# Two of the last block's four half-width output stores moved from SyncE's DMA queue to GpSimd's

## The chip, the cores and the metric

The kernel runs on one core of one Trainium2 chip. The metric is the device time of one launch in microseconds; the figure given for a kernel is the median over several runs. A change of about 0.2% (0.46 us here) is what a measurement of this kernel can tell from none.

## What is computed

A pooled attention is followed by a feed-forward layer with three maxed branches. q, k and v have the shape (8, 8, 576, 64); the reference comes down to this:

```python
k_p = k.reshape(B, H, Sp, pool, D).mean(axis=3)      # pool = 8, Sp = 72
v_p = v.reshape(B, H, Sp, pool, D).mean(axis=3)
attn = softmax(q @ k_p.T / sqrt(D))
x = (attn @ v_p).transpose(0, 2, 1, 3).reshape(4608, 512)
h = max(x @ w1, x @ w2, x @ w3)                      # 4608 x 768
out = h @ w_out                                      # 4608 x 512, float32
```

The change concerns only how part of `out` gets from SBUF to DRAM.

## The kernel before, in words

The 4608 tokens are worked through in nine blocks of 512 (NB). For each block the attention of the image it falls in gives `xT`, the hidden layer gives `hT` (the first branch is subtracted from the two others and added back later through `wm`, so that two products and a max remain), and a projection gives `out`. Blocks 0 to 5 use plain matmuls (`hidden`, line 363, and `project`, line 381). From block 6 on the hidden layer is computed by a scheme with seven products instead of eight on half-size pieces (`seven`, line 698). For the last block, block 8 (`LAST`), the projection is also done by seven products instead of eight (`out_seven`, line 638), at the very end of the kernel; it treats the block's 512 tokens as two halves j = 0 and 1 of 256, each in two groups of 128 tokens, m = 0 and 1.

The order of instructions is written out by hand: each engine runs its own queue in the order in which the program issues to it, and an instruction waits on semaphores for its inputs. DMAs to DRAM are issued by whichever engine's queue the program names: `nc.sync` (SyncE, "SPq" in the profile), `nc.scalar` (ScalarE's queue, "ACTq") or `nc.gpsimd` (GpSimd, "POOL").

The end of the program (lines 802 to 812) is this. Of the plain projection's tiles (blocks 5 to 7, 128 tokens each) two steps are taken first (lines 804 and 805), which end one such tile. Then `fold_h` makes sums of pieces of `hT`, and `outs(i, m)` runs fourteen products in the order given on line 808. Each product is five accumulating matmuls (line 670) into PSUM tiles `oA`, `oB` or `oC`. Products 1, 5, 6 and 3 are copied to the SBUF tile `ob` (called `o` in the code) by ScalarE (`copy`, line 675); products 2, 4 and the pair 5 and 7 are added onto it by VectorE (`plus`, line 678). `ob` is 128 partitions by 2 token halves j, by 2 groups m, by 512 columns of float32. When all that feeds a piece is there, `store` (line 645) sends it out, in two DMAs, one for partitions 0 to 63 (u = 0) and one for 64 to 127 (u = 1), since the two halves go to different rows of `out`:

- "lo": j = 0, columns 0 to 255, after product (2, 1), issued from GpSimd (line 686): two DMAs of 128 KB.
- "j1": j = 1, all 512 columns, after product (3, 1), issued from SyncE (line 694): two DMAs of 256 KB.
- "hi": j = 0, columns 256 to 511, after product (4, 1), issued from SyncE (line 690): two DMAs of 128 KB. These are the two that the change moves.

After the fourteen products the rest of `tiles` runs (line 811): the last plain projection tile (`last` on line 385), cut into two column halves. The first half ("c0") is copied from PSUM to `osb` by ScalarE (line 400), the second ("c1") by VectorE (line 398), and each is stored by two DMAs of 64 KB: u = 0 from SyncE's queue, u = 1 from ScalarE's (line 404). The kernel's last instructions, on line 838, wait on SyncE for every DMA semaphore, one wait after another, and then bring all engines together in a barrier that GpSimd collects.

The SyncE and ScalarE DMAs take their completion semaphore from one set of eight in turn, GpSimd's from another set of eight.

Of the kernel before, what the change touches and what calls it, by code (L numbers as in the profile page):

```python
# [14 lines left out]
def kernel(  # L15
# [11 lines left out]
    nc = tc.nc  # L27
# [34 lines left out]
    def psum(shape, dtype, name, tag, bufs):  # L62
        return pools[-1].tile(shape, dtype, name=name, tag=tag, bufs=bufs)
# [529 lines left out]
    def turns(n):  # L593
        return (pad3 if n % 2 else pad)[:, 0:4]
# [16 lines left out]
    def out_w(z, r):  # L611

        i, j = divmod(z, 2)
        c = slice(HALF * i, HALF * i + HALF)
        return wm_sb[:, 2 * j + r, c] if r < 2 else wo_sb[:, JH * j + r - 2, c]

    def out_s(z):
        return so["S4"][:, 0:5] if z == 4 else so["S123"][:, 5 * z - 5:5 * z]
# [19 lines left out]
    def out_seven(n):  # L638

        o = sb2.tile([128, 2304], F32, name="ob", tag="et")[:, 0:2048].rearrange(  # L640
            "p (j m c) -> p j m c", j=2, m=2)
        lo, hi = slice(0, HALF), slice(HALF, C)
        banks, done = {}, set()

        def store(e, j, c):
            for u in range(2):
                b, g = divmod(2 * (4 * n + 2 * j) + u, NG)
                dst = out[S * b:S * b + S, :].rearrange("(r g) c -> r g c", g=NG)
                e.dma_start(out=dst[:, GS[g]:GS[g + 2] + 1:4, c],
                            in_=o[64 * u:64 * u + 64, j, :, c])  # L650

        def product(i, m):
            of = "B" if i == 2 else "C" if i in (4, 7) else "A"
            if i in FIRST:
                tag = {"A": PA, "B": SC, "C": BC if m == 0 else SC}[of]
                banks[of, m] = psum([128, 2, HALF], F32, name=f"o{of}", tag=tag[0],
                                    bufs=tag[1])
            p = banks[of, m][:, 0]
            za, zb = PRODUCTS[i]
            for r in range(5):  # L660
                c = slice(128 * m, 128 * m + 128)
                if isinstance(zb, str):
                    z = int(zb[1]) - 1
                    left = turns(n)[:, z, r, c] if r < 2 else th[n][:, z, r - 2, c]
                else:
                    at = HALF * (zb % 2) + 128 * m
                    left = (xT[:, 2 * (zb // 2) + r, NB * n + at:NB * n + at + 128] if r < 2
                            else hTs[n][:, JH * (zb // 2) + r - 2, at:at + 128])
                right = out_s(int(za[1]))[:, r] if isinstance(za, str) else out_w(za, r)
                nc.tensor.matmul(p, left, right, start=(i in FIRST and r == 0), stop=(r == 4),  # L670
                                 skip_group_check=True)
            done.add((i, m))

            def copy(j, c):
                nc.scalar.copy(out=o[:, j, m, c], in_=p)

            def plus(j, c, p):
                nc.vector.tensor_tensor(out=o[:, j, m, c], in0=o[:, j, m, c], in1=p,
                                        op=ALU.add)

            if i in (1, 5, 6, 3):
                copy(i in (5, 3), lo if i in (1, 3) else hi)
            elif i == 2:
                plus(0, lo, p)
                if m:
                    store(nc.gpsimd, 0, lo)
            elif i == 4:
                plus(0, hi, p)
                if m:
                    store(nc.sync, 0, hi)  # L690
            if i in (5, 7) and (12 - i, m) in done:
                plus(1, hi, banks["C", m][:, 0])
            if i in (5, 7, 3) and all((z, m) in done for z in (5, 7, 3) for m in range(2)):
                store(nc.sync, 1, slice(0, C))

        return product
# [146 lines left out]
```

The softmax here doesn't subtract the row's maximum and nothing guards it: scores larger than these inputs give would overflow.

## Time and profile before

| what | value |
|---|---|
| median of 5 runs | 230.79 us (230.74 to 231.25) |
| the profiled execution itself | 230.88 us |
| its span in the profile | 229.2 us (229.17 in the trace); 1.7 us lie around it |
| TensorE busy | 218.9 us, 96% of the span |
| GpSimd (POOL) busy | 140.0 us, 61%; nothing between 201.8 and 218.2 us |
| DMA queue q0 (GpSimd), q1 (SyncE), q10 (ScalarE) | 16.98, 16.13 and 0.13 MB |
| stores of `ob` | two from POOL, four from SyncE |
| stores at line 404 | 62 of 128 KB from SyncE; at the end two of 64 KB from SyncE and two from ScalarE |

Times in the profile are in us from the start of the span, of one execution. "PE" is TensorE, "DVE" VectorE, "ACT" ScalarE, "POOL" GpSimd, "SPq" and "ACTq" the queues of SyncE and ScalarE that issue DMAs. The time of a DMA instruction on a queue is the time for which it holds that queue; the bytes move later, and the DMA has landed when all sixteen DMA engines have raised its semaphore. A wait that ends late is put down to what ended it.

### The profile page before, as it was taken

Reading aid. Unit: us, or ns where it says so; the run is one execution under the profiler, and the core shown is the slowest. Engines: PE = TensorE matmul, PEld = TensorE weight load, DVE = VectorE, ACT = ScalarE, POOL = GpSimd, SP = SyncE. Lnnn points to the kernel's source line nnn. Section 1 sums busy time; section 2 is a strip of 40 time slices with the busy share of each in tenths; the row PEclk is TensorE's granted clock in tenths of the full one; section 3 lists DMA queues with packets and bytes.
Section 4 is the critical chain, followed back from the end, with each engine's and each line's share of the span. In section 5 each row is a group of like instructions: output and inputs, shape, how many; then the busy total and the mean of one; then the engine's idle time right before and its main releaser. Section 6 shows DMA issues by size and latency. Waiting matters only on the chain.

```text
span 229.2 us, 4411 instructions
## 1 busy us (share of the span) xinstructions
PE 218.9 (96%) x1686; PEld 134.5 (59%) x1687; DVE 129.9 (57%) x246; ACT 122.7 (54%) x221; POOL 140.0 (61%) x115
## 2 busy tenths in 40 slices
PE   7688999999999999999999999999999999999992
PEld 2467645558656545544554455455678667786682
DVE  3568876038426333632363236368578887897830
ACT  2277424756864586238623862684776435465330
POOL 7974201999959999999999749900343442920020
PEclk9999999999999999999999999999999999999999
DMA  6999999999569999887998799941421534301336
GB/s 160 212 197 197 209 205 208 199 179 225 104 111 218 225 170 205 155 185 118 224 166 195 122 217 193 190 110 24 92 60 30 122 72 88 82 12 46 74 69 183
DMA packets 47157, 33.52 MB, mean 146 GB/s; under 512 B 27104, under 2 KB 41888, under 8 KB 47136
## 3 DMA queue, kind: packets, MB, share of 16 engines
q0 software_dynamic: 16944, 16.98, 45.8%
q1 hardware_dynamic: 30032, 16.13, 31.5%
q8 instruction: 13, 0.21, 0.4%
q10 hardware_dynamic: 160, 0.13, 0.2%
q14 instruction: 8, 0.07, 0.1%
HBM read 34.60 MB, written 9.44 MB: 192 GB/s over the span
## 4 chain that ended last, share of the span: by engine, by line
PE 83%; DVE 5%; DMA 4%; ACT 3%; issue 2%; POOL 1%; DVEq 0%; ACTq 0%; POOLq 0%
PE pw L346 23%; PE po L395 18%; PE po L391 11%; PE pA L733 6%; PE psc L207 5%; PE pav L255 4%; DMA vt<-in_v_dram 4%; PE pC L733 3%; PE pm L333 2%; PE oA L670 2%; PE pB L733 2%; DVE kz L198 2%; DVE xn L263 2%; ACT kz L198 2%; PE pxt L245 1%
## 5 line engine op out<-in xcount | busy, mean ns | idle before, releaser
L346 PE MATMUL pw<-xT,mw 128*128 128x512 f16 (+1 forms) x336 | 73.1, 348 | 0.4 <-ACT xT L249 0.2
L395 PE MATMUL po<-mwo,hT 128*128 128x512 f16 (+1 forms) x198 | 46.8, 372 | 0.0
L354 DVE TENSOR_TENSOR hT<-t,pw 128x512 f16<-128x512 f16 (+1 forms) x42 | 25.5, 610 | 36.7 <-ACT et L212 19.1
L346 PEld LDWEIGHTS <-mw 128*128 128x128 f16 x336 | 31.6, 98 | 21.5 <-DVE mw L319 0.6
L400 ACT COPY osb<-po 128x512 f32<-128x512 f32 (+1 forms) x32 | 18.6, 580 | 41.2 <-PE po L395 40.3
L212 ACT ACTIVATE et<-psc 72x576 f16<-72x576 f32 (+2 forms) x54 | 35.2, 661 | 7.1 <-PE psc L207 7.0
L151 POOL TENSOR_TENSOR half<-vt 72x2048 f32<-72x2048 f16 x7 | 28.4, 4060 | 13.7 <-DMA vt<-in_v_dram 13.3
L391 PE MATMUL po<-wm,xT 128*128 128x512 f16 (+1 forms) x132 | 33.0, 372 | 0.3 <-ACT osb L400 0.3
L352 ACT ACTIVATE t<-pw 128x512 f16<-128x512 f32 (+1 forms) x42 | 22.6, 537 | 13.3 <-PE pw L346 11.5
L263 DVE TENSOR_TENSOR xn<-pav,rcp 128x512 f16<-128x512 f32 x40 | 27.7, 692 | 1.6 <-DVE rcp L261 0.2
L395 PEld LDWEIGHTS <-hT 128*128 128x128 f16 x198 | 18.5, 98 | 16.3
L152 POOL TENSOR_TENSOR half<-half 72x1024 f32<-72x1024 f32 (+1 forms) x13 | 27.3, 2098 | 1.0
L207 PE MATMUL psc<-qT,kz 128*128 128x320 bf16 (+2 forms) x120 | 22.9, 278 | 1.8 <-DVE qT L184 0.9
L207 PEld LDWEIGHTS <-kz 128*128 128x128 bf16 x143 | 13.1, 98 | 14.7 <-ACT kz L198 2.0
L151 POOL TENSOR_TENSOR half<-ktFalse 96x1536 f32<-96x1536 f16 x6 | 18.6, 3098 | 4.6 <-DMA ktFalse<-in_k_dram 4.4
L255 PEld LDWEIGHTS <-et 72*128 72x128 f16 x320 | 15.4, 98 | 7.7 <-issue 0.4
L739 ACT CAST pad<-pA 128x512 f16<-128x512 f32 x27 | 15.4, 588 | 8.4 <-PE pA L733 6.0
L261 DVE RECIPROCAL rcp<-pav 128x8 f32<-128x8 f32 x40 | 8.2, 206 | 18.1 <-PE pav L255 17.9
L391 PEld LDWEIGHTS <-xT 128*128 128x128 f16 x132 | 12.1, 97 | 9.4 <-issue 0.4
L255 PE MATMUL pav<-vp,et 72*128 72x65 f16 x320 | 16.9, 194 | 0.1
L714 DVE SCALAR_TENSOR_TENSOR hT<-pad 128x512 f16<-128x512 f16 x18 | 14.4, 810 | 1.8 <-ACT pad L743 1.4
L733 PEld LDWEIGHTS <-sw 128*128 128x128 f16 x144 | 13.7, 98 | 2.7
(106 smaller groups left out, 277.3 us busy)
## 6 DMA issues: line engine op xcount, KB each, us to landing
out_dram<-osb SPq DMA_DIRECT2D x62, 128.0 KB, 3.0
ktFalse<-in_k_dram POOLq DMA_DIRECT2D x7, 576.0 KB, 6.8
qb<-in_q_dram POOLq DMA_DIRECT2D x7, 576.0 KB, 13.0
vt<-in_v_dram POOLq DMA_DIRECT2D x7, 576.0 KB, 11.4
mw<-in_moe_w_dram POOLq DMA_DIRECT2D x9, 256.0 KB, 9.3
ktTrue<-in_k_dram SPq DMA_DIRECT2D x3, 384.0 KB, 5.3
mwo<-in_moe_w_out_dram POOLq DMA_DIRECT2D x1, 768.0 KB, 13.3
qb<-in_q_dram POOLq DMA_DIRECT2D x2, 288.0 KB, 7.9
```

The costliest lines, as they stand in the source:

```text
L151: e.tensor_tensor(out=f, in0=t[:, :, 0:4, :], in1=t[:, :, 4:8, :], op=ALU.add)
L152: e.tensor_tensor(out=f[:, :, 0:2, :], in0=f[:, :, 0:2, :], in1=f[:, :, 2:4, :], op=ALU.add)
L207: nc.tensor.matmul(out, kz_all[b % 2][f % 2][:, h, :], qTs[b][:, n + i0:n + i1, 64 * (h % 2):64 * (h % 2) + 64], start=True, stop=True)
L212: nc.scalar.activation(out=out, in_=in_, func=FT.Exp, scale=1.0 / 64.0)
L255: nc.tensor.matmul(pav[:, h // 4, 65 * (h % 4):65 * (h % 4) + 65], ets[b][:, h, c0:c0 + 128], vp_all[:, b, h, :], start=True, stop=True)
L263: nc.vector.tensor_tensor(out=xn, in0=pv[:, :, :, 0:D], in1=rcp.to_broadcast([128, 2, 4, D]), op=ALU.mult)
L346: mm = nc.tensor.matmul(pw, w_sb[wi][:, kc, bass.ts(jc, 128)], xT[:, kc, col], start=(kc == 0), stop=(kc == KCH - 1))
L352: nc.scalar.activation(out=t, in_=pw, func=FT.Relu)
L354: nc.vector.tensor_tensor(out=hT[:, jc, c0:c1], in0=t, in1=pw, op=ALU.max)
L391: nc.tensor.matmul(po, xT[:, kc, bass.ts(m, 128)], wm_sb[:, kc, c], start=(kc == 0), stop=False)
L395: nc.tensor.matmul(po, hT[:, jc, bass.ts(mm, 128)], wo_sb[:, jc, c], start=False, stop=(jc == JCH - 1))
L733: mm = nc.tensor.matmul(p[:, w], a[:, kc, bass.ts(g, 128)], b[:, kc, :], start=(i in FIRST and w + kc == 0), stop=(w + kc == 2), skip_grou ...
```

## The change

In `out_seven`, the store of columns 256 to 511 of token half j = 0 is issued from GpSimd's queue instead of SyncE's. Being called once for m = 1, it is two DMA instructions. Nothing else is edited.

```diff
             elif i == 4:
                 plus(0, hi, p)
                 if m:
-                    store(nc.sync, 0, hi)
+                    store(nc.gpsimd, 0, hi)
             if i in (5, 7) and (12 - i, m) in done:
```

In the compiled order TensorE, VectorE and ScalarE have the same instructions in the same order. GpSimd has two more DMAs after the two "lo" stores that were already its last, ahead of its end of program. SyncE loses two DMAs between the "j1" stores and the last two stores of line 404. Those last two stores on SyncE now take the completion semaphores that the "hi" stores had; the two on ScalarE keep theirs.

## The prediction

> **What bounds the kernel now.** I read the chain of waits at the end first, then the instructions in order of time from 222 us, then the DMA share by stretch, then the end of the program.
>
> ```profile
> 222.87 0.44 PE po L391 x4
> 223.31 0.66 PE po L395 x6
> 223.96 0.44 PE po L391 x4
> 224.40 0.67 PE po L395 x6
> 225.07 0.02 issue
> 225.09 0.42 DVE osb L398
> ```
>
> The chain (start, duration, what) is TensorE without a gap to 225.07, then the copy of c1, the last tile's second column half, on VectorE to 225.52. The stores follow. No edit here touches TensorE, VectorE or ScalarE, so everything to 225.52 stays. What can move lies in the 3.65 us from there to the span's end at 229.17.
>
> ```profile
> 222.22 2.88 SPq L649 DMA_DIRECT2D out_dram<-ob  x4
> 224.40 1.63 ACTq L404 DMA_DIRECT2D out_dram<-osb  x2
> 225.19 1.34 SPq L404 DMA_DIRECT2D out_dram<-osb  x2
> ```
>
> This is the timeline of the two queues. SyncE's four stores of `ob` are j1 at 222.22 and 222.91, then hi at 223.62 (held 0.60 us) and 224.27 (held 0.83). Behind them wait its two stores of `osb`: c0 at 225.19, though ScalarE issued its half of c0 at 224.40, and c1 at 225.99, though ScalarE issued its half of c1 at 225.55. So hi makes SyncE 0.79 us late with c0 and 0.44 us late with c1. That is all that the change can give back.
>
> ```profile
> 223.50:225.00 1.50, 1.50 (x15) 1.15 (x12) 0.00 (x0) 0.37 (x1) 0.00 (x0) 1.00 0.94 201
> 225.00:226.00 1.00, 0.06 (x1) 0.00 (x0) 0.42 (x1) 0.00 (x0) 0.00 (x0) 1.00 0.96 291
> 226.00:227.00 1.00, 0.00 (x0) 0.00 (x0) 0.00 (x0) 0.00 (x0) 0.00 (x0) 1.00 0.87 275
> 227.00:227.75 0.75, 0.00 (x0) 0.00 (x0) 0.00 (x0) 0.00 (x0) 0.00 (x0) 1.00 0.74 243
> ```
>
> The last two columns of the stretches are the busy share of the sixteen DMA engines and GB/s. From 223.5 to 227.75 these engines are nearly full: 1 MiB of stores goes through, whoever issued it, and there is little idle time to win.
>
> Who waits for the landings? On line 838 SyncE waits for the semaphores one after another, 0.06 us each. In the trace's semaphore records ScalarE's c1 lands at 228.01, and the waits after it pass at 228.03, 228.09, 228.15, 228.21 and 228.27; SyncE's c1 lands at 228.18, just before its turn at 228.21. The list is through at 228.33, the barrier follows, and the span ends 0.84 us later. So two landings bind at once: ScalarE's c1 plus 0.32, and SyncE's c1 plus 0.15.
>
> ```profile
> L838 POOLq EVENT_SEMAPHORE  x4: 17/17/17, 228.4 to 229.1; - x4
> L838 POOLq DRAIN  x3: 51/102/3172, 218.7 to 228.9; - x3
> ```
>
> These are two rows of the end of the program (min/median/max ns, first and last start). GpSimd's first drain takes 3.17 us: it follows its two lo stores and ends at 221.87, unseen, since GpSimd enters the barrier only at 228.42. After the change this cover shrinks.
>
> **What the Trainium skill says.** "DMA: Bandwidth & Descriptors", section "Issuing engines are not separate DMA queues": DMAs from several engines run on the same 16 DMA engines, and issuing from more of them saves only the issue time. The trace agrees: full engines above, 0.79 and 0.44 us of issue. The same page, "SWDGE vs HWDGE vs iDMA": each DMA engine serves its queues in turn, a packet at a time, of at most 4096 bytes. The packet records show 4096-byte packets for GpSimd's lo stores, against 1024 bytes for hi from SyncE. Same page, "Latency and other measured facts": first byte after some 0.6 us from SyncE, 1 us from GpSimd. Here the trace differs: first packet 1.31 us after the start of SyncE's first j1 (222.22 to 223.52), 1.22 after that of GpSimd's first lo (218.25 to 219.47). I use these. "Perfetto Trace Analysis", section "DMA Instruction — HWDGE (DVE, Sync)": two queues share one descriptor generator under a lock. The trace fits: the second hi, overlapped by ScalarE's c0, held SyncE 0.83 us, the first, alone, 0.60.
>
> **The change part by part.**
>
> *SyncE loses two DMAs.* It is free after j1 at 222.91 + 0.62 = 223.53. c0 can then go when its copy ends (224.00 + 0.37 = 224.37), so at 224.40, with ScalarE's; c1 at 225.55, with ScalarE's. c0 gains 0.79, c1 0.44. SyncE's c1 landed 2.19 us after issue, so would land at 227.74 instead of 228.18 if it kept that latency. But ScalarE's c1, which is not issued earlier, decides too.
>
> *ScalarE's c1.* Issue stays at 225.55; only its latency can change, 2.46 us now. Lower bound: the 2.19 of SyncE's c1, of the same 64 KB, which went out last as the traffic ebbed: 227.74. Upper bound: the 2.76 of ScalarE's c0 in the thick of it: 228.31. By volume: from 224.81, where j1's first store is through, 768 KB remained and took to 227.72. They cannot end much earlier, since at 225.55 + 1.3 = 226.85, when c1's first packets can flow, about 70 KB of backlog should still be there (294 KB moved by 225.07, then about 300 KB per us, of 896 KB issued). 70 + 128 KB at that rate is 0.65 us: 227.5. Landing came 0.53 us after ScalarE's last packet before (227.48 to 228.01): about 228.0. Between this and the lower bound I take 227.92. SyncE's c1 now goes out at the same moment and shares the generator's lock (up to 0.24 us for one of the two, by the 0.83 against 0.60); I take it to land together with ScalarE's.
>
> *The order of the final waits.* SyncE's c1 takes over a semaphore of hi, which stands right behind ScalarE's c1 in the list; three more follow. So its landing is now followed by 0.26 us of list, not 0.15. The list ends at 227.92 + 0.32 = 228.24 instead of 228.33: a gain of 0.09 us.
>
> *GpSimd gains two DMAs.* Its last work before is lo, issued by 219.52, so nothing is queued behind hi but the drain. Its wake-up is slower: lo began 0.31 us after the VectorE add that releases it, where SyncE needs 0.03. hi's data is ready at 222.91 + 0.42 = 223.33, so the stores start at 223.64 and 224.28 (0.64 each): as on SyncE (223.62, 224.27), so neither gain nor loss. First packets at 224.86 and 225.6. GpSimd's packets took 300 ns per 4096 bytes while TensorE ran; 1024-byte packets of SyncE took a median of 46 ns after it had stopped. Per DMA engine hi is 16 KB: 4 x 300 = 1.2 us against 16 x 46 = 0.74. Upper bound of that cost 0.46 us, lower bound 0, since no row shows GpSimd's packets without TensorE beside them; 2048-byte ones sped up from 145 to about 85 ns, so I take 0.
>
> *The drain.* It ended 2.34 us after the second lo was issued (219.52) and 0.45 after it landed (221.41). By the first reading it ends at 224.92 + 2.34 = 227.26; by the second, with hi landing as late as 227.40 as now, at 227.85. Both lie ahead of 228.42, so I cost it at 0. If that cover goes, the end moves by what the drain passes 228.42.
>
> *Sum.* 0.09 us less for the profiled execution: 230.88 - 0.09 = 230.79. It stood 0.09 over the median of 230.79, so the median goes to 230.70. With c1's two bounds (-0.27 and +0.30): 230.52 to 231.09.
>
> **The rivals.** About 0.2%, 0.46 us, is what a measurement of this kernel can tell from no change.
>
> *A, the forecast: full DMA engines hide the gain.* For it: shares of 0.94 to 0.74. Against: SyncE's c1 alone would be 0.44 earlier. 230.70, chance 0.60.
>
> *B: the traffic clears before c1.* Packets from GpSimd mix in from 224.86, and c1 meets empty queues: 1.31 to its first packet, 0.25 for its bytes, 0.46 to land is 2.0 us, so 227.55, 0.46 earlier: 230.3. For it: 0.87 and 0.74 show slack after 226. Against: 768 KB in 2.7 us needs all of it. Chance 0.15.
>
> *C: GpSimd's drain ends last.* If those 2.34 us are work left per issued DMA (1.17 each), four DMAs make 4.7 us: 224.92 + 4.7 = 229.6, against 228.42: 1.2 us slower, 232.0. It decides from the point where the drain passes 228.42. For it: the 3.17 us drain is the longest instruction of the end. Against: lo was long done when hi comes, and 221.87 fits the landing as well. Chance 0.18.
>
> *D: GpSimd's larger packets fill the DMA engines.* The 0.46 us bound above, with half of it on c1's way: 230.79 + 0.25 = 231.04, within 0.2%. Chance 0.07.
>
> **How the numbers follow.** B is faster by over 0.2%: 0.15. A and D are within: 0.67. C is slower: 0.18. The range covers A with its own bounds, B and D, from 230.3 to 231.2, and leaves C out.
>
> **What would show it.** Right: SyncE's stores of c0 and c1 start near 224.40 and 225.55, GpSimd's near 223.64 and 224.28; ScalarE's c1 lands between 227.74 and 228.31; the DMA share stays above 0.85 to 227; the drain ends before 228.2. Wrong: GpSimd's drain ends after the last landing and the barrier follows it at once (C), a c1 landing before 227.6 (B), or packets of q0 still moving after 227 (D).

## The result, and the profile after

The change makes the kernel slower: 231.47 us (median of 43 runs) against 230.83 us (median of 80 runs), a ratio of 1.0027 with a 95% interval of 1.0019 to 1.0035. That is 0.64 us more; forecast were 0.09 us less and a range that ended at 231.2 us.

The profiled execution of the changed kernel has a span of 231.3 us, but 1.5 us of that have nothing to do with the change: its TensorE clock was granted at 0.91 in the first 20 us, and everything after lies later by as much. So I measure from a mark that both have, the start of VectorE's copy of c1: 225.09 us before, 226.58 us after. From there to the end of the span ("the tail") it is 4.07 us before and 4.73 us after. The 0.66 us between them is the whole loss. Times "from the mark" below count from that copy's start.

The timeline of the queues and of the copies of the changed kernel:

```profile
223.70 1.32 SPq L649 DMA_DIRECT2D out_dram<-ob  x2
223.85 0.97 DVE L678 TENSOR_TENSOR ob<-ob,oC 128x256 f32<-128x256 f32 x2 [1.15 <-PE oC L670]
225.11 1.20 POOL L649 DMA_DIRECT2D out_dram<-ob  x2 [4.10 <-DVE ob L678]
225.49 0.37 ACT L400 COPY osb<-po 128x256 f32<-128x256 f32 x1 [1.81 <-PE po L395]
225.89 1.64 SPq L404 DMA_DIRECT2D out_dram<-osb  x2
225.89 1.65 ACTq L404 DMA_DIRECT2D out_dram<-osb  x2
226.58 0.42 DVE L398 COPY osb<-po 128x256 f32<-128x256 f32 x1 [1.76 <-PE po L395]
```

The issue side is what the change promised. SyncE and ScalarE send c0 together at 225.89 (0.69 before the mark) and c1 together at 227.03 (0.45 after it); before, SyncE's were at 0.10 and 0.89 after the mark. GpSimd starts hi 1.47 us before the mark, as SyncE had.

What came of it is in the landings. These are the issues in two narrow windows, around c1's issue on ScalarE before the change, and around c1's issue on both queues after it (kind, count, KB, us to landing; SyncE's row in the first is c0, still being issued):

```profile
out_dram<-osb SPq DMA_DIRECT2D x1, 64.0 KB, 2.7
out_dram<-osb ACTq DMA_DIRECT2D x1, 64.0 KB, 2.5
```

```profile
out_dram<-osb SPq DMA_DIRECT2D x1, 64.0 KB, 2.9
out_dram<-osb ACTq DMA_DIRECT2D x1, 64.0 KB, 3.1
```

ScalarE's c1 is issued 0.46 us after the mark in both kernels, and needs 3.10 us instead of 2.46. These 0.64 us are the loss. Most of it, 0.52 us, is in the passage of the packets: its last one ends 2.91 us after the mark instead of 2.39. The rest lies between that packet and the landing, 0.65 us instead of 0.53. From its landing to the end of the final list of waits it is 0.32 us in both.

Where do the stores lose the time? These are stretches of the changed kernel, and under them those of the kernel before, cut at the same distances from the mark. The last two columns are the busy share of the 16 DMA engines and GB/s:

```profile
225.00:226.50 1.50, 1.50 (x15) 1.14 (x12) 0.00 (x0) 0.37 (x1) 1.20 (x2) 1.00 0.94 203
226.50:227.08 0.58, 0.04 (x1) 0.00 (x0) 0.42 (x1) 0.00 (x0) 0.00 (x0) 1.00 0.97 325
227.08:227.58 0.50, 0.00 (x0) 0.00 (x0) 0.00 (x0) 0.00 (x0) 0.00 (x0) 1.00 0.57 184
227.58:228.00 0.42, 0.00 (x0) 0.00 (x0) 0.00 (x0) 0.00 (x0) 0.00 (x0) 1.00 0.95 315
228.00:229.00 1.00, 0.00 (x0) 0.00 (x0) 0.00 (x0) 0.00 (x0) 0.00 (x0) 1.00 0.79 246
229.00:229.75 0.75, 0.00 (x0) 0.00 (x0) 0.00 (x0) 0.00 (x0) 0.00 (x0) 0.98 0.34 113
```

```profile
223.52:225.02 1.50, 1.50 (x15) 1.13 (x12) 0.00 (x0) 0.37 (x1) 0.00 (x0) 1.00 0.95 203
225.02:225.60 0.58, 0.04 (x1) 0.00 (x0) 0.42 (x1) 0.00 (x0) 0.00 (x0) 1.00 1.01 307
225.60:226.10 0.50, 0.00 (x0) 0.00 (x0) 0.00 (x0) 0.00 (x0) 0.00 (x0) 1.00 0.84 256
226.10:226.52 0.42, 0.00 (x0) 0.00 (x0) 0.00 (x0) 0.00 (x0) 0.00 (x0) 1.00 0.84 278
226.52:227.52 1.00, 0.00 (x0) 0.00 (x0) 0.00 (x0) 0.00 (x0) 0.00 (x0) 1.00 0.91 287
227.52:228.27 0.75, 0.00 (x0) 0.00 (x0) 0.00 (x0) 0.00 (x0) 0.00 (x0) 1.00 0.13 42
```

As j1 runs out, 0.5 us after the mark, there is a hole: a share of 0.57 where it was 0.84, though hi and c0 have long been issued. The packet records tell what kind of loss it is. From the first packet of j1 to the last of c1, the packets kept one DMA engine busy for 3.70 us on average after the change, against 3.78 us before (the sum over all packets, divided by 16): GpSimd's packets are not dearer. But that work is spread over 4.48 us instead of 4.20, so an engine is idle for 0.77 us instead of 0.42. In the hole, 0.8 to 1.1 us after the mark, about eight of sixteen engines work (9 to 11 in a repeat of the kernel); eight of the sixteen engines raise the semaphore of GpSimd's first hi store by 1.55 us, eight only from 2.02.

The end of the program, after (min/median/max ns, first and last start):

```profile
L838 POOLq EVENT_SEMAPHORE  x4: 17/17/17, 230.6 to 231.2; - x4
L838 POOLq DRAIN  x3: 51/106/4581, 225.5 to 231.0; - x3
```

GpSimd's drain is now 4.58 us long and ends at 230.12, 0.54 us after the second hi store landed (before: 0.46 after the second lo store). The barrier comes at 230.57, so the drain is still covered, by 0.45 us.

### The profile page after: what moved, and what is told of

Its sections match the earlier page's. It is cut to its first block, busy times and chain, and to the rows that moved or that the text cites. A ratio compares the mean times of both kernels' runs of the same rounds, so it can differ in the third digit from the quotient of the medians.

```text
span 231.3 us, 4410 instructions
## 1 busy us (share of the span) xinstructions
PE 220.1 (95%) x1686; PEld 135.5 (59%) x1687; DVE 130.3 (56%) x246; ACT 122.6 (53%) x221; POOL 141.4 (61%) x117
## 4 chain that ended last, share of the span: by engine, by line
PE 84%; DVE 6%; ACT 3%; DMA 3%; issue 2%; SPq 0%; DVEq 0%; ACTq 0%
PE pw L346 23%; PE po L395 17%; PE po L391 11%; PE pA L733 6%; PE psc L207 6%; PE pav L255 4%; PE pC L733 3%; DMA ktTrue<-in_k_dram 3%; PE pm L333 2%; PE oA L670 2%; PE pqt L182 2%; PE pB L733 2%; DVE kz L198 2%; DVE xn L263 2%; ACT kz L198 1%
## 5 line engine op out<-in xcount | busy, mean ns | idle before, releaser
L207 PE MATMUL psc<-qT,kz 128*128 128x320 bf16 (+2 forms) x120 | 23.5, 284 | 1.8 <-DVE qT L184 0.9
```

The costliest lines, as they stand in the source:

```text
L207: nc.tensor.matmul(out, kz_all[b % 2][f % 2][:, h, :], qTs[b][:, n + i0:n + i1, 64 * (h % 2):64 * (h % 2) + 64], start=True, stop=True)
```

## The experiments

There were two theories. Theory P: GpSimd's hi stands in the DMA engines' way when c0 and c1 want to pass. Theory I: it is the issuing of c0 and c1 from two queues in the same instant that makes both slow. The cuts of code below are against the changed kernel; the versions whose name ends in "_sync" make the same edit in the kernel before, with hi from SyncE. In the table, "issued" is c1 on SyncE / ScalarE from the mark, "landed" how long each took from there, by the semaphore records of one execution (between repeats of one kernel they and the tail differ by up to 0.15 us); the ratio is to the kernel before on the same chip.

| kernel | c1 issued | c1 landed after | tail | median us | ratio (95%) |
|---|---|---|---|---|---|
| before | 0.89 / 0.46 | 2.19 / 2.46 | 4.07 | 230.83 | 1 |
| changed | 0.45 / 0.46 | 2.92 / 3.10 | 4.73 | 231.47 | 1.0027 (1.0019 to 1.0035) |
| after_again | 0.45 / 0.46 | 2.85 / 3.04 | 4.65 | 231.79 | 1.0042 (1.0030 to 1.0054) |
| no_hi | 0.45 / 0.46 | 1.96 / 2.20 | 3.83 | 230.45 | 0.9988 (0.9977 to 0.9999) |
| hi_scalar | 1.35 / 1.38 | 2.03 / 2.29 | 4.70 | 231.49 | 1.0030 (1.0018 to 1.0042) |
| one_each | 0.45 / 0.46 | 2.58 / 2.74 | 4.36 | 231.05 | 1.0008 (0.9994 to 1.0021) |
| hi_half_gps | 0.45 / 0.46 | 2.29 / 2.50 | 4.12 | 230.82 | 1.0003 (0.9991 to 1.0015) |
| hi_half_sync | 0.90 / 0.46 | 2.00 / 2.10 | 3.89 | 230.57 | 0.9997 (0.9984 to 1.0010) |
| four_first_gps | 0.45 / 1.03 | 2.32 / 2.07 | 4.33 | 231.38 | 1.0027 (1.0016 to 1.0039) |
| four_first_sync | 0.53 / 0.86 | 2.69 / 2.52 | 4.50 | 231.49 | 1.0029 (1.0015 to 1.0043) |
| split_gps | 0.45 / 0.46 | 1.97 / 2.24 | 3.73 | 230.47 | 0.9989 (0.9977 to 1.0001) |
| split_sync | 0.91 / 0.46 | 2.00 / 2.10 | 4.27 | 230.96 | 1.0010 (1.0001 to 1.0020) |
| four_first_split | 0.45 / 1.07 | 1.97 / 2.25 | 4.36 | 231.36 | 1.0016 (1.0004 to 1.0027) |
| split_gps_again | 0.45 / 0.46 | 2.12 / 2.32 | 3.83 | 230.44 | 0.9982 (0.9971 to 0.9994) |

**The changed kernel again.** No edit.

> The changed kernel once more, for its tail on the same chip as the three others. All theories: 231.4 us, ratio 1.002 to 1.0035, a tail of about 4.7 us from the start of VectorE's c1 copy to the end, hi landing after 2.9 us or more, GpSimd's drain ending about 0.5 us after the second hi store has landed and before the barrier.

As expected in all but the size: 1.0042, a little over the foreseen ratio, and a tail of 4.65 us.

**Without hi.**

```diff
             elif i == 4:
                 plus(0, hi, p)
-                if m:
-                    store(nc.gpsimd, 0, hi)
```

> The two hi stores are left out altogether (256 KB of the output are never written); SyncE and ScalarE still issue c0, and then c1, in the same instant. Theory P (GpSimd's hi packets stand in the DMA engines when c0 and c1 want to pass): without them c1 lands some 2.0 to 2.2 us after its issue, the tail from the start of VectorE's c1 copy to the end of the span is 3.6 to 3.9 us, against 4.07 before and 4.73 after, so 230.3 to 230.7 us. Theory I (issuing c0 and c1 from two queues in the same instant makes both slower, in the shared descriptor generator): c1 still takes 2.6 us or more, the tail stays above 4.2 us and the time above 230.9 us.

c0 and c1 still leave both queues together, and c1 lands after 1.96 and 2.20 us, the tail is 3.83 us. The issues around c1 in this run:

```profile
out_dram<-osb SPq DMA_DIRECT2D x1, 64.0 KB, 2.0
out_dram<-osb ACTq DMA_DIRECT2D x1, 64.0 KB, 2.2
```

So the joint issue by itself is not slow, which Theory I said it is. (Whether it is slow with hi's bytes beside it, `one_each` below answers.) It also gives a price of hi on ScalarE's c1: 2.20 us with none, 2.46 with hi from SyncE (0.26 more), 3.10 with hi from GpSimd (0.90 more). These two prices are not of the queue alone, since with hi from SyncE that queue's c0 and c1 leave later too. In this run c0's first packets on SyncE's queue flow 0.52 us after the mark and on ScalarE's 0.81; in the changed kernel they start at 1.05 and 1.51, while engines idle. So GpSimd's stores hold back packets of other queues that would otherwise flow.

**hi from ScalarE's queue.**

```diff
-                    store(nc.gpsimd, 0, hi)
+                    store(nc.scalar, 0, hi)
```

> The two hi stores go to ScalarE's queue in place of GpSimd's: off SyncE as in the change, but without GpSimd's software queue. Theory P: the extra time goes, c1 lands at most 2.5 us after its issue, the tail is 3.9 to 4.2 us, the time 230.6 to 231.0 us, as before the change. Theory I: SyncE and ScalarE still issue c1 in the same instant and hi beside j1, so the time stays near 231.4 us.

By its time, 231.49 us, this spoke for Theory I. Its profile says otherwise:

```profile
223.25 1.98 ACTq L649 DMA_DIRECT2D out_dram<-ob  x2
225.75 1.14 SPq L404 DMA_DIRECT2D out_dram<-osb  x2
225.75 1.41 ACTq L404 DMA_DIRECT2D out_dram<-osb  x2
```

ScalarE was held 1.98 us by hi, 1.31 of them by the first store; only then could it copy c0, and c1 left at 1.35 to 1.38 us from the mark, 0.92 us later than in the changed kernel. From its issue c1 took 2.03 and 2.29 us, as Theory P has it, though so late an issue also meets less traffic. It is the same time from another cause: late issue instead of slow passage. My forecast for the time failed, because I had left out what ScalarE has queued behind hi.

**One hi store from each queue.**

```diff
-                e.dma_start(out=dst[:, GS[g]:GS[g + 2] + 1:4, c],
+                (e[u] if isinstance(e, tuple) else e).dma_start(out=dst[:, GS[g]:GS[g + 2] + 1:4, c],
...
-                    store(nc.gpsimd, 0, hi)
+                    store((nc.gpsimd, nc.sync), 0, hi)
```

> The first hi store (partitions 0 to 63) goes from GpSimd, the second (64 to 127) from SyncE. Theory P with a cost by bytes: half of the 0.6 us, so about 231.1 us. P with a cost that comes with any hi packet of GpSimd in the tail: about 231.4 us. Theory I: SyncE is free at about the same time for c0 as in the change, so c0 and c1 go out together and the time is that of the change, 231.4 us or more.

It took 231.05 us, and 2.74 us for ScalarE's c1. This is the cleanest comparison of queues here: SyncE and ScalarE issue c0 and c1 at the same moments as in the changed kernel, the bytes are the same, and only one of the two hi stores comes from another queue (for which it leaves 0.60 us earlier; no run takes that apart). That takes 0.36 us off ScalarE's c1 (3.10 to 2.74), and the medians of one chip differ by 0.74 us (231.79 in `after_again`, 231.05 here). Theory I forecast 231.4 us or more, and fails again.

**Half of hi's columns, from GpSimd and from SyncE.**

```diff
-                    store(nc.gpsimd, 0, hi)
+                    store(nc.gpsimd, 0, slice(HALF, HALF + HALF // 2))
```

> The changed kernel, but GpSimd's two hi stores send 128 of their 256 columns (the other 128 columns are left out of the output): the same number of DMAs and of rows, half the bytes and so half of the 4096-byte packets. If the cost goes with the bytes or packets that GpSimd puts among the others, c1 lands 2.7 us after its issue in place of 3.0 to 3.1 and the time is 0.3 us less than the changed kernel, about 231.1 us. If it goes with the number of DMAs or rows, c1 stays at 3.0 us and the time at 231.4 us. If nothing but the volume counted, it would lie halfway between the 230.45 without hi and the time of the change.

> The kernel before with the same half of hi left out, from SyncE: the control for the halved store from GpSimd. 128 KB less in the tail: c1 of ScalarE lands 2.3 us after its issue in place of 2.46; but SyncE still issues its c1 at the same late moment, whose 2.0 to 2.2 us then ends the kernel, so 230.6 to 230.75 us. If the cost of GpSimd goes with bytes, the gap between the two halved kernels is 0.3 us, half of that of the whole ones; if with DMAs or rows, 0.6 us.

With as many DMAs and rows but half the bytes, the two kernels differ by 0.25 us (230.82 and 230.57), their tails by 0.23 us, where the whole ones differ by 0.64 and 0.66. On ScalarE's c1 the gap is 0.40 us (2.50 and 2.10), where it was 0.64. So the cost falls with the bytes, that is with the number of 4096-byte packets, 64 to 32; whether in proportion, these two measures don't agree, and the intervals of the two medians overlap. A cost by the number of DMAs, which stayed, would have left the gap near 0.64. c1's 2.50 us and the 230.82 us are below what I expected of a cost by bytes (2.7 and 231.1); the time is also a little below halfway between no hi and the change (230.96).

**hi ahead of j1.**

```diff
-                 (7, 1), (3, 0), (3, 1), (4, 0), (4, 1)):
+                 (7, 1), (4, 0), (4, 1), (3, 0), (3, 1)):
```

> The changed kernel with products (4,0), (4,1) ahead of (3,0), (3,1), so that hi is ready about 1.1 us earlier, leaves from GpSimd ahead of j1, and passes the DMA engines while nothing else is on them. Theory P1 (GpSimd's packets cost only where they meet others that end the kernel, here c0 and c1): c1 lands at most 2.4 us after its issue, tail 3.8 to 4.1 us, 230.4 to 230.8 us, the extra 0.6 us is gone. Theory P2 (the last GpSimd stores cost some 0.6 us wherever they are in the last microseconds, by the drain or the software's own work): 231.2 us or more.

> The kernel before with the same swap of products, hi from SyncE ahead of j1: the control for the run before it. Both theories: the same bytes in the tail in another order, SyncE still late with c0 and c1 as before, so within 0.15 us of before, 230.6 to 230.9 us. P1 expects the version with GpSimd to be level with this one or up to 0.3 us faster, P2 expects it 0.5 us slower.

Both missed their times for the same reason, which no forecast had. In the version with GpSimd:

```profile
222.67 1.20 POOL L649 DMA_DIRECT2D out_dram<-ob  x2 [3.21 <-DVE ob L678]
223.44 1.31 SPq L649 DMA_DIRECT2D out_dram<-ob  x2
224.61 2.27 ACTq L404 DMA_DIRECT2D out_dram<-osb  x2
224.85 1.43 SPq L404 DMA_DIRECT2D out_dram<-osb  x2
```

ScalarE's store of c0 at 224.61 held its queue 1.63 us (1.46 in the control), so its c1 left at 1.03 instead of 0.46. Still, the pair answers its question: with GpSimd's hi ahead of the others, SyncE's c1, which leaves at 0.45 as in the changed kernel, takes 2.32 us instead of 2.92, and the kernel is not slower than its control with SyncE (231.38 and 231.49 us). P2, a cost that goes with GpSimd's late stores as such, expected 0.5 us more.

**j1 in two parts.**

```diff
-            if i in (5, 7, 3) and all((z, m) in done for z in (5, 7, 3) for m in range(2)):
-                store(nc.sync, 1, slice(0, C))
+            if i in (5, 7) and all((z, m) in done for z in (5, 7) for m in range(2)):
+                store(nc.sync, 1, hi)
+            if i == 3 and m:
+                store(nc.sync, 1, lo)
```

> The changed kernel with j1 cut in two: its columns 256 to 511 leave from SyncE as soon as products 5 and 7 are summed, about 1 us earlier than now, its columns 0 to 255 after product 3 as now. Half of j1's bytes are then gone before hi comes. If GpSimd's hi costs because it meets j1's backlog and, through that, c0 and c1, hi now passes before c0, c1 lands 2.2 to 2.4 us after its issue, the tail is 3.8 to 4.0 us and the time 230.5 to 230.7 us, 0.1 to 0.3 us under the kernel before. If its cost does not need the backlog, c1 still takes 2.8 us or more and the time is 231.1 us or more.

> The kernel before with j1 cut in the same way, hi from SyncE: the control. SyncE issues c1 as late as before (0.89 us after the start of VectorE's c1 copy), and with the lighter traffic it lands 2.0 to 2.2 us later, so the tail is 3.85 to 4.05 us and the time 230.6 to 230.8 us. By the theory of the backlog the version with GpSimd is level or up to 0.1 us faster; if GpSimd's cost needs no backlog, it is 0.3 us or more slower.

With half of j1 sent 1 us earlier, GpSimd's hi meets less of a backlog (its first packet comes 1.50 us after issue, not 2.14) and is through before c1 comes: c1 takes 1.97 and 2.24 us, as if there were no hi at all (2.12 and 2.32 in the repeat), and the tail is 3.73 us. The stretches of this kernel, at the distances from the mark used above:

```profile
224.95:225.53 0.58, 0.03 (x1) 0.00 (x0) 0.42 (x1) 0.00 (x0) 0.00 (x0) 1.00 0.89 293
225.53:226.03 0.50, 0.00 (x0) 0.00 (x0) 0.00 (x0) 0.00 (x0) 0.00 (x0) 1.00 0.77 193
226.03:226.45 0.42, 0.00 (x0) 0.00 (x0) 0.00 (x0) 0.00 (x0) 0.00 (x0) 1.00 0.84 271
226.45:227.45 1.00, 0.00 (x0) 0.00 (x0) 0.00 (x0) 0.00 (x0) 0.00 (x0) 1.00 0.63 184
```

GpSimd's price has not gone: c0 takes 2.75 and 2.93 us here, against 2.06 and 2.25 without hi. But c0 does not end the kernel. The control with SyncE is slower than I expected, 230.96 us, and its records say why: its own c1 lands 2.91 us from the mark, early enough, but its semaphore is the second in the final list, and seven more waits of 0.06 us follow, 0.42 us in all. In the version with GpSimd only two waits follow that of the last landing. So of the 0.54 us between the two tails, 0.31 us is the order of a list, and 0.22 us the later landing of SyncE's c1.

**hi first and j1 in two parts.** Both edits above, on the changed kernel.

> The changed kernel with both the swap of products (hi ahead of j1's second part) and j1 cut in two: only 256 KB of j1 remain in the tail with c0 and c1. If ScalarE's issue of c0 is held 1.3 us or more whenever it comes within 0.5 us of SyncE's second store of j1, it is held here too, c1 leaves late from ScalarE (at 0.8 us or more after the start of VectorE's c1 copy, not 0.46) and the tail is 4.0 us or more, 230.8 us or more. If what holds it is the 2048-byte rows of j1 (1024 here), it is held 0.5 to 0.6 us, c1 leaves at 0.46, lands 2.2 us later, and the time is 230.4 to 230.6 us, the best of all.

ScalarE's c0 was held again, 1.66 us, with 1024-byte rows too, and c1 left at 1.07. So the 2048-byte rows of j1 are not what holds it. Nor is it enough that a SyncE store leaves just ahead of it: in split_sync one of hi's left 0.41 us before ScalarE's c0, which was held 0.56 us; in the kernel before, one left 0.14 us before, and it was held 0.55 us.

**The best version, again.**

> The changed kernel with j1 cut in two, once more, since its first interval only just reached 1: does it beat the kernel before? By the tail of 3.73 us against 4.07 it should be 0.34 us faster: ratio 0.9985, 230.45 us. If the first result was chance, the ratio lies within 0.0005 of 1.

230.44 us, 0.9982 (0.9971 to 0.9994): GpSimd's queue for hi, with j1 in two parts, beats both kernels, the one before by about 0.4 us. Not all of that is passage: of the 0.34 us between the tails of the kernel before and split_gps, 0.22 us is the earlier landing of ScalarE's c1 (2.69 from the mark instead of 2.91) and 0.12 us its place in the final list (0.20 us of list behind it instead of 0.32).

## Why the prediction was wrong

- **SyncE's issue times** were right: c0 and c1 at -0.69 and 0.46 from the mark were forecast, -0.69 and 0.45 came. That the gain of SyncE's c1 is worth little as long as ScalarE's is not earlier was right too. The 0.24 us that I allowed for the lock of a shared generator did not come: c1's two stores, sent together, held their queues 0.49 and 0.50 us.
- **"ScalarE's c1"** is the step that failed. I bounded its landing between 2.19 and 2.76 us after its issue, by two stores of the kernel before, and took 2.37. It took 3.10. Both of those stores had passed beside traffic of SyncE's and ScalarE's queues alone; no row of the kernel before had GpSimd's packets among others in the tail, so neither was a bound for what the change makes.
- **"GpSimd gains two DMAs"**: the start was right (-1.47 and -0.87 came, -1.45 and -0.81 forecast), the passage wrong. I had put the first packet 1.22 us after issue, at -0.23 from the mark, mixed into j1. It came at 0.67, 2.14 us after issue, when j1 was nearly through (at 0.15 in the repeat, 1.62 us after issue). And I priced hi by how long its packets keep an engine busy, between 0 and 0.46 us, and took 0. That price was right: the packets took 159 ns, not 300, and busy time did not rise. What rose is idle time between packets, 0.35 us per engine, for which I had no term at all.
- **By volume**: I reckoned that full engines finish 768 KB at the same time whoever sends it. They were not full: 0.57 in the hole. Nor was the 0.53 us from c1's last packet to its landing a constant; it was 0.65 us.
- **The Trainium skill's sentence** that DMAs from several engines share the same 16 DMA engines, and that more queues save only issue time ("DMA: Bandwidth & Descriptors", "Issuing engines are not separate DMA queues"), I read as "the bytes pass as fast from any queue". The runs contradict that reading: one of the two hi stores from SyncE's queue instead of GpSimd's, at the same issue times of c0 and c1, made ScalarE's c1 0.36 us faster (`one_each`).
- **The order of the final waits** was right in kind and size for this change (0.32 us from ScalarE's landing in both); split_sync shows that the list can cost 0.42 us.
- **The drain** (rival C) was harmless, though C named the right direction of the time. It ends with the landing (0.46 and 0.54 us after), not by work per DMA, which by C's sum would have ended it 4.5 us from the mark; it ended at 3.54, with the barrier at 3.99.
- **Rival D** came nearest: packets of GpSimd still moved 2.4 us from the mark, its sign. But its mechanism, packets that fill the engines, is refuted by the busy time; and its whole bound of 0.46 us is less than the 0.64 us that c1 lost.
- **Rival B** is what split_gps shows: once the traffic clears before c1, c1 lands in 2.0 to 2.2 us.

What stays open: why a DMA engine stands idle when it has GpSimd's packets and others waiting. That c0's packets were held back while about half the engines idled is shown; whether the engines wait for GpSimd's descriptors is only a guess, and no run here looks inside an engine. Nor does a run separate GpSimd's queue from the size of its packets, 4096 bytes against 1024 for hi from SyncE. One other cause can be set aside: VectorE's copy of c1, from 0 to 0.42 us after the mark, does not stop GpSimd's packets, which flow from 0.15 us in after_again and from 0.03 us in split_gps.

## What to carry to other kernels

Near the end of this kernel, a store was to be priced by what it does to the latency of the store that lands last, not by its issue time or its bytes; a bound for that has to come from traffic of the same mix of queues. Moving a store to an idle engine's queue paid here only after the backlog ahead of it was sent earlier, so that it was through before the last store came. And two kernels with the same time can have different causes: look at when the last store is issued and how long it takes, separately.

## What was not expected of the hardware

- ScalarE's DMA instruction held its queue 1.31 to 1.66 us in four kernels (hi_scalar and the three with hi first), 0.48 to 0.58 us in most others. In these four, an 8 KB transfer on the instruction queue q14 had begun 0.03 to 0.53 us before it, and the hold ended 1.66 to 1.84 us after the transfer's start; in the others that transfer came at least 1.1 us earlier. That the queue waited for its own instructions fits, but no run took the transfer away.
- The position of a semaphore in the final list of waits mattered: in split_sync 0.42 us of waits followed that of the last store to land, in split_gps 0.12 us.
- GpSimd's drain follows the landing of its last store, by 0.46 to 0.54 us.
